# The first two weight loads of a decode block change queues, and one of them is issued in two pieces

## The chip, the cores and the metric

The kernel runs on one core of a Trainium2 chip. The metric is the device time of one execution in microseconds (us), the median of the timed runs. On the core, TensorE (PE), VectorE (DVE), ScalarE (ACT), GpSimd (POOL) and SyncE (SP) each have their own instruction stream. Data comes from the chip's main memory (HBM) into the on-chip memory SBUF, which has 128 partitions, by 16 DMA engines. SP and ACT each issue transfers into a queue of their own; the profile calls SP's queue q1 and ACT's q10.

## The reference

One decode step of a transformer block for 4 sequences (one new token each, width 512, float32), with the modulation of an adaptive layer norm:

```python
mod = (_silu(c) @ w_mod).reshape(c.shape[0], 6, 1, -1)
sa, ca, ga, sb, cb, gb = (mod[:, n] for n in range(6))
h = _layernorm(x) * (1 + ca) + sa
x = x + ga * _A_ref(h, A_k_cache, A_v_cache, A_wq, A_wo)
h = _layernorm(x) * (1 + cb) + sb
x = x + gb * _B_ref(h, B_w1, B_w3, B_w2)
# _A_ref: q = h @ wq (32 heads of 128); 8 key/value heads, the last 2048 positions of
#         the cache; softmax(q k / sqrt(128)) v; the heads' outputs @ wo
# _B_ref: (silu(h @ w1) * (h @ w3)) @ w2, inner width 1792
```

In all the kernel reads 101 MB, of which wq is 8.3 MB and the first part of w_mod (the columns for sa and ca, with x and c beside them) 2.1 MB.

## The kernel before

The host lays all inputs out as tiles of 128 partitions, so that each load is one wide transfer. SBUF holds a `ring` of three slots of 65,536 bytes for each partition. The loads go through it in a fixed order that is written out by hand:

- `w_mod_a` (128 rows of 16,512 bytes) into slot 0 and `wq` (128 rows of 64,576 bytes) into slot 1, both at the start;
- `guests`: the last 240 columns of wq, which are left out of the `wq` tile, as 24 rows of 5,760 bytes into the tile `p_sb`, in eight transfers of three rows. In each transfer the rows go to partitions four apart (`c`, `c+4`, `c+8`, or these plus 32). They wait for Pool's memset of `p_sb`;
- `kv_in[0]` to `kv_in[6]` (keys and values of one key/value head for all four sequences, 128 rows of 65,536 bytes) into slots 2, 0, 1, 2, ..., each issued when the slot's last reader is done;
- `wo_mod`, `last_k_wo`, `last_v`, `wo`, `w1`, `w3` and four pieces of `w2` into freed parts of the ring.

All loads but `wq` are issued by SP in that order; `wq` is issued by ACT (`queue="scalar"`). The helper is

```python
def load(dst, src, cuts=(0, 1), queue="sync"):
    step = src.shape[1] // cuts[-1]
    for lo, hi in zip(cuts[:-1], cuts[1:]):
        do(queue, "dma_start", dst[:, lo * step : hi * step], src[:, lo * step : hi * step])
    return dst[:, : src.shape[1]]
```

The computation follows the loads. When w_mod_a has landed, ACT and DVE form silu(c) (tiles `e`, `sc`), Pool copies x (`xs`), PE transposes and averages it and multiplies `sc` with w_mod_a (`bank<-ring,sc`); DVE makes the normalised, modulated `h`, and PE its transpose `hT`. From here slot 0 is free and `kv_in[1]` is issued. Then PE multiplies `hT` with wq (`s_ps<-ring,hT`), and slot 1 is free for `kv_in[2]`. Eight groups follow, one for each key/value head: scores (`s_ps<-ring,qT`), maximum (`nm`), exponential (`p_sb`), transposes, product with the values (`o_ps`). Then come the projection with wo, the second norm, and the gated layer with w1, w3 and w2.

`Program` (`do(...)`) records every operation with the SBUF and PSUM ranges that it reads and writes, works out the waits itself, and emits the instructions for each engine in the recorded order. For that reason nearly every instruction carries the one line L59 in the profile, and rows are told apart by their tiles. Each transfer has a semaphore of its own.

Of the kernel before, what the change touches and what calls it, by code (L numbers as in the profile page):

```python
# [9 lines left out]
P = 128  # L10
# [137 lines left out]
def block_kernel(nc, w_mod_a, wq, guests, kv_in, wo_mod, last_k_wo, last_v, wo, w1, w3, w2, out):  # L148
# [5 lines left out]
    do = Program(nc)  # L154
# [8 lines left out]
    slots = [ring[:, n * 2 * HALF : (n + 1) * 2 * HALF] for n in range(3)]  # L163
# [10 lines left out]
# [5 lines that stand above are left out]
# [4 lines left out]

    first = load(slots[0], w_mod_a)
    wma, xt_sb, ct_sb = first[:, :4096], first[:, 4096:4112], first[:, 4112:]
    wq_t = load(slots[1], wq, queue="scalar")
    do("scalar", "preload_act_table_set", "natural_log_exp_and_others")
    kv = [None] * G  # L190

# [347 lines left out]
```

## Time and profile before

| What | Value |
|---|---|
| timed runs | 242.05, 242.22, 242.52 us; median 242.22 |
| the profiled execution | span 240.8 us from its first to its last instruction; the median is 1.4 us above it |
| PE busy | 148.7 us, 62% |
| DVE, ACT, POOL busy | 56.3, 24.1, 4.5 us |
| SP's queue (q1) | 92.99 MB, 89.8% of 16 DMA engines' span |
| ACT's queue (q10) | 8.27 MB, 8.0% |
| read from HBM | 101.22 MB, 420 GB/s over the span |
| from issue to landing | w_mod_a 26.7 us, wq 26.9 us |

The profiled execution has no time of its own outside its span; the runs' times hold the span and what lies around it. The shares of the queues say how long their packets kept the 16 DMA engines busy, as a part of 16 times the span. The chain that ended last is 60% DMA, 31% PE, 5% DVE and 3% ACT. In views of a stretch, a DMA packet is counted where it starts.

### The profile page before, as it was taken

The numbers are of one execution on the slowest core, as the hardware profiler recorded it, in microseconds if no ns is written. First come the engines' busy times: TensorE is split into PE (matmuls) and PEld (weight loads), VectorE is DVE, ScalarE is ACT, GpSimd is POOL, SyncE is SP. The second block draws the span as 40 slices with busy tenths as digits, with TensorE's granted clock in tenths as the row PEclk, the third lists the DMA queues.
The fourth block names the chain that finished last, engine by engine and source line by source line (L and its number), as shares of the span: only waits on it lengthen the run. The fifth ranks groups of instructions, "written<-read, shape, count | busy, mean of one in ns | idle before, by whom it ended". The sixth has DMA issues, their size and how long they took to land.

```text
span 240.8 us, 2502 instructions
## 1 busy us (share of the span) xinstructions
PE 148.7 (62%) x1113; PEld 54.2 (22%) x1113; DVE 56.3 (23%) x141; ACT 24.1 (10%) x36; POOL 4.5 (2%) x12
## 2 busy tenths in 40 slices
PE   0000169982984962944867576667399719965876
PEld 0000133322322212201312222221042202422333
DVE  5000231034152024123132133130313104113210
ACT  2000000003003003001100300300200001320100
POOL 7000000000000000000000000000000000000000
PEclk9999997997696798879797799795759968995899
DMA  8999999999999999999999999999999999999994
GB/s 305 434 444 455 424 425 446 416 446 414 457 395 468 403 459 414 449 425 446 425 446 427 435 435 435 435 427 446 425 446 425 411 419 430 386 444 443 401 413 162
DMA packets 2937, 101.39 MB, mean 421 GB/s; under 512 B 472, under 2 KB 472, under 8 KB 880
## 3 DMA queue, kind: packets, MB, share of 16 engines
q1 hardware_dynamic: 2784, 92.99, 89.8%
q10 hardware_dynamic: 144, 8.27, 8.0%
q8 instruction: 8, 0.13, 0.2%
q14 instruction: 1, 0.01, 0.0%
HBM read 101.22 MB, written 0.03 MB: 420 GB/s over the span
## 4 chain that ended last, share of the span: by engine, by line
DMA 60%; PE 31%; DVE 5%; ACT 3%; issue 1%; ACTq 0%
DMA ring<-kv_in 33%; DMA ring<-w 16%; PE s_ps L59 14%; DMA ring<-w_mod_a 11%; PE bank L59 9%; PE o_ps L59 6%; DVE nm L59 3%; ACT p_sb L59 3%; PE a_ps L59 1%; DVE mod_a L59 0%; ACT work L59 0%; DVE p_sb L59 0%; DVE e L59 0%; DVE h L59 0%; DVE sq L59 0%
## 5 line engine op out<-in xcount | busy, mean ns | idle before, releaser
L59 PE MATMUL s_ps<-ring,qT 128*32 128x512 f32 x256 | 36.5, 722 | 20.3 <-DMA ring<-kv_in 13.3
L59 PE MATMUL bank<-ident,p_sb 128*128 128x128 f32 (+1 forms) x136 | 27.7, 353 | 30.8 <-ACT p_sb L59 30.7
L59 PE MATMUL o_ps<-ring,pT 128*16 128x512 f32 x256 | 38.4, 707 | 0.1
L59 PEld LDWEIGHTS bank<-ident,p_sb 128*128 128x128 f32 (+1 forms) x136 | 19.8, 178 | 52.5 <-ACT p_sb L59 31.7
L59 ACT ACTIVATE p_sb<-s_ps,nm 128x2048 f32<-128x2048 f32 (+1 forms) x11 | 16.5, 1501 | 139.7 <-DVE oT L59 104.1
L59 DVE TENSOR_REDUCE nm<-s_ps 128x1 f32<-128x2048 f32 x7 | 16.0, 2292 | 32.5 <-PE s_ps L59 32.5
L59 DVE COPY pT<-bank 128x64 f32<-128x64 f32 x32 | 7.2, 225 | 57.0 <-PE bank L59 57.0
L59 PEld LDWEIGHTS s_ps<-ring,qT 128*32 128x32 f32 x256 | 8.7, 129 | 46.9 <-issue 20.1
L59 PE MATMUL bank<-ident,xs 128*128 128x128 f32 x1 | 0.5, 476 | 27.8 <-POOL xs L59 27.8
L59 PE MATMUL s_ps<-ring,h2T 128*32 128x512 f32 (+1 forms) x64 | 9.0, 657 | 2.3 <-DMA ring<-w 2.3
L59 PE MATMUL s_ps<-ring,hT 128*32 128x512 f32 (+1 forms) x64 | 9.4, 705 | 0.0
L59 PEld LDWEIGHTS o_ps<-ring,pT 128*16 128x16 f32 x256 | 5.4, 99 | 11.9 <-issue 9.0
L59 DVE SCALAR_TENSOR_TENSOR o_own<-o_ps,rl,own 128x512 f32<-128x512 f32 x7 | 5.3, 751 | 11.1 <-PE o_ps L59 11.1
L59 PE MATMUL a_ps<-ring,oT 128*4 128x512 f32 x64 | 7.4, 592 | 0.0
L59 DVE TENSOR_REDUCE o_sum<-o_own 128x128 f32<-128x512 f32 x7 | 7.2, 1034 | 0.2
L59 PE MATMUL bank<-ring,sc 128*32 128x256 f32 (+1 forms) x64 | 6.9, 587 | 0.0
L59 PEld LDWEIGHTS bank<-ident,xs 128*128 128x128 f32 x1 | 0.2, 183 | 27.8 <-POOL xs L59 27.8
L59 DVE TENSOR_SCALAR e<-e 128x16 f32<-128x16 f32 x1 | 0.2, 175 | 23.3 <-ACT e L59 23.3
L59 DVE COPY qT<-bank 128x64 f32<-128x64 f32 x8 | 2.2, 280 | 12.4 <-PE bank L59 12.0
L59 DVE TENSOR_REDUCE mx<-s_ps 128x1 f32<-128x512 f32 x4 | 2.8, 692 | 9.0 <-PE s_ps L59 9.0
L59 PEld LDWEIGHTS s_ps<-ring,h2T 128*32 128x32 f32 x64 | 2.6, 130 | 7.3 <-issue 4.4
L59 PE MATMUL s_ps<-ring,hidT 128*32 128x64 f32 (+1 forms) x112 | 3.6, 274 | 0.3 <-DVE hidT L59 0.3
(97 smaller groups left out, 63.7 us busy)
## 6 DMA issues: line engine op xcount, KB each, us to landing
ring<-wq ACTq DMA_DIRECT2D x1, 8072.0 KB, 26.9
ring<-w SPq DMA_DIRECT2D x2, 3584.0 KB, 37.9
ring<-last_k_wo SPq DMA_DIRECT2D x1, 6144.0 KB, 30.1
ring<-last_v SPq DMA_DIRECT2D x1, 4096.0 KB, 39.5
ring<-w_mod_a SPq DMA_DIRECT2D x1, 2064.0 KB, 26.7
ring<-wo SPq DMA_DIRECT2D x1, 2048.0 KB, 41.8
ring<-w SPq DMA_DIRECT2D x1, 2048.0 KB, 43.1
ring<-w SPq DMA_DIRECT2D x1, 768.0 KB, 44.5
```

The source lines that it names most:

```text
L59: op = Op(engine, lambda: getattr(getattr(self.nc, engine), method)(*args, **kw), [])
```

## The change

SP now issues wq, in two transfers: the first 16 partitions, and then the other 112. ACT issues w_mod_a. Both happen at the start, ahead of everything else on the two queues. What is loaded, and to which addresses, stays the same.

```diff
-    first = load(slots[0], w_mod_a)
+    wq_t = slots[1][:, : wq.shape[1]]
+    for lo, hi in ((0, 16), (16, P)):
+        do("sync", "dma_start", wq_t[lo:hi], wq[lo:hi])
+    first = load(slots[0], w_mod_a, queue="scalar")
     wma, xt_sb, ct_sb = first[:, :4096], first[:, 4096:4112], first[:, 4112:]
-    wq_t = load(slots[1], wq, queue="scalar")
     do("scalar", "preload_act_table_set", "natural_log_exp_and_others")
```

On SP, at the start of the program, the transfers stand like this, with a minus as they were and with a plus as they are now (tile written, tensor read, partitions x elements):

```order
@@ -1,3 +1,4 @@
-L59 DMA ring<-w_mod_a 128x4128
+L59 DMA ring<-wq 16x16144
+L59 DMA ring<-wq 112x16144
 L59 DMA p_sb<-guests 3x1440 x8
 L59 DMA ring<-kv_in 128x16384 x7
```

The guests and the key/value loads now stand behind two transfers of wq on SP's queue instead of one of w_mod_a.

On ACT, also at its start (the table load is for the exponential; `e` is the first work that reads w_mod_a's tile):

```order
@@ -1,3 +1,3 @@
-L59 DMA ring<-wq 128x16144
+L59 DMA ring<-w_mod_a 128x4128
 L59 ACT_TABLE_LOAD
 L59 ACTIVATE e<-ring 128x16
```

The one transfer on ACT's queue is now w_mod_a. The other engines' instructions stand as they did; PE's first product with `hT` waits for two transfers of wq where it waited for one.

## The prediction

> **What bounds the kernel now.** I read the page's slices first, then the stretches of the span, then the chain and the DMA issues. The slices and queues of the page:
>
> ```profile
> span 240.8 us, 2502 instructions
> DMA  8999999999999999999999999999999999999994
> q1 hardware_dynamic: 2784, 92.99, 89.8%
> q10 hardware_dynamic: 144, 8.27, 8.0%
> ```
>
> q1 is SP's queue, q10 ACT's, which carries wq alone. Together their packets fill 97.8% of what 16 DMA engines have in the span. The stretches (third column from the right: granted TensorE clock; then DMA share and GB/s; a packet counts where it starts, so a short stretch can show over 1):
>
> ```profile
> 0.00:1.70 1.70, 0.00 (x0) 0.00 (x0) 0.73 (x3) 0.55 (x1) 0.94 (x7) 1.00 0.00 0
> 28.20:47.00 18.80, 15.52 (x120) 6.26 (x120) 3.68 (x15) 1.06 (x3) 0.00 (x0) 0.91 1.00 433
> 47.00:181.00 134.00, 90.01 (x568) 31.72 (x566) 35.94 (x66) 15.01 (x15) 0.00 (x0) 0.82 1.00 433
> 181.00:229.00 48.00, 34.08 (x263) 11.78 (x259) 11.38 (x36) 5.32 (x14) 0.00 (x0) 0.86 0.99 423
> 237.70:240.80 3.10, 1.09 (x64) 0.75 (x53) 0.45 (x2) 0.00 (x0) 0.00 (x0) 1.00 0.05 11
> ```
>
> Nothing moves for 1.7 us; then the engines run without a gap, at 433 GB/s (27.1 GB/s each), until the last weights have come at 237.7, and 3.1 us of work follow. So the kernel is one stream of 101 MB, and a microsecond that the DMA engines lose anywhere in it is a microsecond at the end, because no later stretch has idle time to win it back. The chain ends the same way: it hands over from transfer to transfer, and its first and last long pieces are
>
> ```profile
> 0.73 26.68 DMA ring<-w_mod_a
> 190.94 38.54 DMA ring<-w
> ```
>
> The change touches the first of them. Its two transfers, in the timeline and in the list of issues:
>
> ```profile
> 0.73 0.39 ACTq L59 DMA_DIRECT2D ring<-wq  x1
> 0.73 0.38 SPq L59 DMA_DIRECT2D ring<-w_mod_a  x1
> 3.23 5.67 SPq L59 DMA_DIRECT2D p_sb<-guests  x8
> 8.95 25.57 SPq L59 DMA_DIRECT2D ring<-kv_in  x2
> ring<-wq ACTq DMA_DIRECT2D x1, 8072.0 KB, 26.9
> ring<-w_mod_a SPq DMA_DIRECT2D x1, 2064.0 KB, 26.7
> ```
>
> Both land after the same 27 us though one is a quarter of the other. The DMA view of a stretch of 3 us, typical for 5 to 26 us, says why:
>
> ```profile
> DMA packets 32, 1.30 MB, mean 432 GB/s; under 512 B 0, under 2 KB 0, under 8 KB 0
> q10 hardware_dynamic: 16, 1.03, 79.5%
> q1 hardware_dynamic: 16, 0.26, 20.5%
> ```
>
> Each engine carries eight rows (partitions) of each tile and takes one row from one queue, then one from the other. A wq row of 64,576 bytes takes 79.5% of 3.0 us, 2.38 us; a w_mod row 0.61 us; eight pairs are 24 us.
>
> **The change, part by part.** Sums are against the profiled execution, 240.8 us; the median of the timed runs, 242.22, stands 1.4 above it, and I add that at the end.
>
> *Issues.* SP issues one transfer more. An issue costs SP 0.38 us, and SP had nothing to do between 1.11 us and the guests at 3.23, which wait for Pool's memset of p_sb: zero, and 0.4 us for the guests and kv_in if that cover were gone. Even then the guests stand behind 20 us of rows on the same queue. ACT issues w_mod_a in place of wq, one for one: zero.
>
> *Order on the engines.* wq, guests and kv_in now share SP's queue, w_mod_a is alone on ACT's. Rows still alternate, so eight pairs still take 24 us and both tiles land together: zero for the landing. kv_in's second load, issued when w_mod's slot is free (8.95 + 25.57 = 34.5 us), has 13 us in hand, as the first keeps the engines busy to about 47.5 (28.2 plus eight rows of 2.42, a kv_in row being 65,536 bytes at 27.1 GB/s). PE's product with hT waits for two transfers of wq instead of one; they end together.
>
> *The start.* The first 5.3 us, in the DMA view (40 slices of 0.13 us):
>
> ```profile
> DMA  0000000000000998030099999900000000000000
> q10 hardware_dynamic: 16, 1.03, 49.8%
> q1 hardware_dynamic: 16, 0.26, 19.8%
> ```
>
> SP's rows start in the fourteenth slice, at 1.7 us, 0.6 us after its issue ended at 1.11; ACT's follow at 2.65. The first w_mod row takes 1.05 us (19.8% of 5.3) instead of 0.61, the first wq row 2.64 instead of 2.38. A transfer of 16 rows could start its rows earlier than one of 128; at most the 0.6 us is to be won. ACT's w_mod rows may come a microsecond late, but the engines have a wq row of 2.4 us by then. I take zero and keep -0.6 for the range.
>
> *The 16 rows.* This is the term that decides. The nearest narrow transfers are the guests, eight of three rows, whose rows stand four partitions apart. The DMA view of 27.1 to 28.1 us holds four of them alone (slices of 25 ns):
>
> ```profile
> GB/s 0 0 0 0 461 231 0 0 0 0 0 0 0 461 231 0 0 0 0 0 0 0 461 231 0 0 0 0 0 0 0 461 231 0 0 0 0 0 0 0
> DMA packets 25, 0.07 MB, mean 69 GB/s; under 512 B 13, under 2 KB 13, under 8 KB 25
> q1 hardware_dynamic: 25, 0.07, 17.2%
> ```
>
> Every 0.22 us three rows of 5,760 bytes start together: each of three engines carries one row. Twelve rows take 17.2% of 16 engine-microseconds, 0.23 us each with the 13 short signal packets counted in, or 25 GB/s: full pace. So I expect 16 rows to go to 16 engines, one each, and 112 to go seven to an engine.
>
> Then all 16 engines write 16 neighbouring partitions at once, a case of which this trace has no row. If engines don't hinder each other there, a row takes 2.38 us: no cost. If partitions share a way into the memory, the guests bound the sharing: rows four apart ran side by side at full pace, so at most four neighbours share one. Four engines on one way take 4 x 2.38 = 9.5 us for their rows, and all 16 engines are held alike, since an engine finishes a row before it takes one of the other queue: +7.1 us. Between 0 and +7.1 I take +7.1: the pace per engine is the same 25 to 27 GB/s for rows of 5.8, 16.5 and 64.6 KB, which looks like a fixed width on each path rather than a common limit at the source, and 128 rows on 16 engines give each path eight partitions of its own.
>
> [...]
>
> *The 112 rows.* Suppose that engine e carries rows 16+7e to 22+7e in order, and that a path's eight partitions are two groups of four, 32 apart. At the first step the engines are at rows 16, 23, 30 ... 121: rows 16 and 51 meet on one path, and 72 and 107. Counted over all seven steps an engine needs between 7 and 10 row times for its seven rows. The latest engine decides when a tile has landed: 3 x 2.38 = +7.1. w_mod's eight rows (4.9 us) stretch on these paths by the same 10 to 7: +2.1. The ends for this part are 0, no meetings, and +50, if the rows were dealt out in turn so that sixteen neighbours are always under way (7 x 7.1).
>
> Sum: 240.8 + 7.1 + 7.1 + 2.1 = 257.1 us; with 1.4 us around it 258.5. All later tiles have 128 rows, so the lag stays what it is.
>
> **Rivals.**
> 1. *The first piece collides, the second doesn't.* Seven rows to an engine may be dealt so that paths stay apart. 242.2 + 7.1 = 249.3. For it: the 128-row tiles run at full pace, however they are dealt. Against: a count of 112 does not split into 16 equal sets of whole groups of four.
> 2. *No collisions: nothing changes.* Bytes, rows per engine and landing order are the same; 242.2. For it: no row of the trace shows an engine held up by another. Against: no row shows a narrow piece of neighbouring rows at full pace either.
> 3. *Faster: the small first transfer starts the stream sooner* and nothing collides. Place: the dead time from 1.11 to 1.7 us. It is worth up to 0.6 us, 241.6, and counts from 0.48 us on. For it: every microsecond at the start is one at the end. Against: ACT's 128 rows came 0.95 us after SP's, which need not shorten with fewer rows on SP.
> 4. *The 112 rows are dealt out in turn:* 242.2 + 7.1 + 50 = 299. Against: in the guests' view one transfer's rows start together on three engines, which fits either way of dealing.
>
> [...]
>
> **How the numbers follow.** Collisions in both pieces 0.57, in the first alone 0.13, dealt in turn 0.04: slower 0.74. No change 0.13. Shorter start 0.13. A run of this kernel tells 0.2%, 0.48 us, from no change. For the likeliest case alone the range is 250 to 264: its low end has few meetings in the second piece, its high end engines that drift out of step and meet longer, by half as much again of the 9.2 us of the second piece. The range to hold 8 in 10 leaves out the shorter start and the turn-wise dealing (0.17) and reaches from no change, 241.8, to 264.
>
> **What would show it.** Collisions: wq and w_mod_a land 10 to 20 us later than 27 us; in the first 12 us SP's queue moves some 110 GB/s; the stretch 47 to 181 keeps 433 GB/s; the tail after the last weights stays 3.1 us. First piece alone: slow to about 11 us, then 432 GB/s. No change: landings at 27 us. Shorter start: first packets well before 1.7 us. I am wrong if the 16 wq rows take 2.4 us each while all engines write neighbours.

## The result, and the profile after

The changed kernel takes 266.46 us (median of 4 runs, 266.07 to 267.08) where the kernel before takes 242.22 (242.05 to 242.52). The ratio is 1.1004, 95% interval 1.0991 to 1.1017: 24.2 us slower. The forecast was slower, 258.5 us, with a range up to 264; the direction and the place are right, the size is 8 us short.

The page of the changed kernel (span, the DMA engines' busy share in 40 slices of 6.6 us, what they moved, the two queues):

```profile
span 264.7 us, 2503 instructions
DMA  9987988899989998999999999999999999999992
GB/s 156 236 196 231 323 211 216 318 455 465 438 386 436 475 438 386 437 465 418 426 426 455 406 428 446 455 406 428 446 455 404 389 455 408 418 442 433 412 406 86
q1 hardware_dynamic: 2800, 99.14, 94.1%
q10 hardware_dynamic: 144, 2.11, 3.2%
```

Read the two slice rows together. The engines count as busy from the start, as before, but in the first eight slices (53 us) they move 156 to 323 GB/s instead of some 430. A row that reads "busy" therefore doesn't say that work is done at full pace; the GB/s row does. The stretches of the changed kernel put the loss into its place (the last two columns are DMA share and GB/s):

```profile
0.00:1.70 1.70, 0.00 (x0) 0.00 (x0) 0.73 (x3) 0.54 (x1) 0.94 (x7) 1.00 0.00 0
1.70:12.60 10.90, 0.00 (x0) 0.00 (x0) 2.65 (x15) 0.74 (x1) 3.33 (x5) 1.00 1.00 143
12.60:50.40 37.80, 0.00 (x0) 0.00 (x0) 0.00 (x0) 0.00 (x0) 0.00 (x0) 1.00 1.02 263
72.00:205.00 133.00, 91.32 (x583) 33.02 (x582) 36.38 (x69) 15.01 (x15) 0.00 (x0) 0.81 1.00 432
261.50:264.70 3.20, 1.16 (x66) 0.94 (x64) 0.45 (x2) 0.00 (x0) 0.00 (x0) 1.00 0.05 12
```

The stream starts at 1.7 us, as before. Up to 12.6 us, while the first 16 rows of wq and 32 of w_mod's 128 are under way, it runs at 143 GB/s; up to 50.4, with the other 112 rows, at 263. From there it has its old pace of 432, and the tail after the last weights is 3.2 us against 3.1. Nothing later gives the loss back. The issues of the changed kernel (KB each, us from issue to landing):

```profile
ring<-wq SPq DMA_DIRECT2D x1, 1009.0 KB, 12.2
ring<-wq SPq DMA_DIRECT2D x1, 7063.0 KB, 50.4
ring<-w_mod_a ACTq DMA_DIRECT2D x1, 2064.0 KB, 50.6
```

The first 16 rows need 12.2 us and both tiles 50 instead of 27: 23.5 and 23.9 us later, and the end is 24.2 us later. PE and DVE do the same work as before (148.6 and 56.3 us busy); they begin later.

How fast single rows go shows in a DMA view of a short stretch of the changed kernel. The first 16 rows of wq are those of 1.7 to 12.6 us (q1's other 16 packets are short signals):

```profile
q1 hardware_dynamic: 32, 1.03, 77.4%
q10 hardware_dynamic: 32, 0.53, 22.6%
```

77.4% of 10.9 us on 16 engines, over 16 rows, are 8.4 us a row. The first rows of the 112 start between 12.65 and 17.6 us:

```profile
DMA packets 32, 1.30 MB, mean 262 GB/s; under 512 B 0, under 2 KB 0, under 8 KB 0
q1 hardware_dynamic: 16, 1.03, 88.0%
q10 hardware_dynamic: 16, 0.26, 21.2%
```

Sixteen wq rows take 88.0% of 4.95 us on 16 engines, 4.36 us each instead of 2.38; sixteen w_mod rows 1.05 us instead of 0.61. Between 23.4 and 26.4 us it is otherwise:

```profile
DMA packets 29, 1.25 MB, mean 416 GB/s; under 512 B 0, under 2 KB 0, under 8 KB 0
q1 hardware_dynamic: 16, 1.03, 98.8%
q10 hardware_dynamic: 13, 0.21, 23.5%
```

Here a wq row takes 2.96 us on the mean, but the trace's single packets show that 14 of the 16 rows take 2.7 us and two take 4.9 and 5.1. In the stretch behind it, 26.7 to 31.6 us, that pace is gone again (80.0% of 4.9 us, 3.92 us a row):

```profile
q1 hardware_dynamic: 16, 1.03, 80.0%
```

So the 112 rows aren't slow evenly. Taken sixteen at a time in the order of their starts, they have means of 4.36, 4.42, 2.96, 3.92, 4.56, 4.48 and 4.22 us by the packets: one step runs at nearly full pace, six at little more than half. The experiments say why.

### The profile page after: what moved, and what is told of

It reads as the page before. It is cut to its first block, busy times and chain, and to the rows that moved or that the text cites. A ratio compares the mean times of both kernels' runs of the same rounds, so it can differ in the third digit from the quotient of the medians.

```text
span 264.7 us, 2503 instructions
## 1 busy us (share of the span) xinstructions
PE 148.6 (56%) x1113; PEld 55.0 (21%) x1113; DVE 56.3 (21%) x141; ACT 24.1 (9%) x36; POOL 4.5 (2%) x12
## 4 chain that ended last, share of the span: by engine, by line
DMA 46%; PE 27%; another core or an unknown queue 18%; DVE 4%; ACT 3%; issue 0%; ACTq 0%
DMA ring<-wo_mod 16%; DMA ring<-w 15%; DMA ring<-kv_in 15%; PE s_ps L59 11%; PE bank L59 8%; PE o_ps L59 6%; DVE nm L59 3%; ACT p_sb L59 3%; PE a_ps L59 1%; ACT L59 0%; DVE mod_a L59 0%; ACT work L59 0%; DVE p_sb L59 0%; DVE e L59 0%
## 5 line engine op out<-in xcount | busy, mean ns | idle before, releaser
L59 PE MATMUL s_ps<-ring,qT 128*32 128x512 f32 x256 | 35.4, 703 | 19.1 <-DMA ring<-kv_in 10.8
L59 PE MATMUL bank<-ident,p_sb 128*128 128x128 f32 (+1 forms) x136 | 28.4, 359 | 30.8 <-ACT p_sb L59 30.7
L59 PEld LDWEIGHTS bank<-ident,p_sb 128*128 128x128 f32 (+1 forms) x136 | 20.6, 184 | 52.7 <-ACT p_sb L59 31.7
## 6 DMA issues: line engine op xcount, KB each, us to landing
ring<-wq SPq DMA_DIRECT2D x1, 7063.0 KB, 50.4
ring<-wq SPq DMA_DIRECT2D x1, 1009.0 KB, 12.2
```

The source lines that it names most:

```text
L59: op = Op(engine, lambda: getattr(getattr(self.nc, engine), method)(*args, **kw), [])
```

## The experiments

Theory P is that of the prediction: engines that write partitions of one path into SBUF at the same time share its pace; a path, as it supposes, serves four neighbouring partitions and the four that lie 32 on. No trace names the path of a packet, so the pairs that meet are counted by this grouping; the landings of the single transfers below fit it (sixteen rows: 5.0 and 5.1 us without a pair, 6.5 to 7.3 with one to eight pairs). The rivals are Q (the new order on the queues costs), S (reading in HBM costs), N (any narrow piece costs), C (a second or small first transfer costs), M (the engines are only set out of step) and, later, H (engines that meet also hold up those that don't).

**Swap and split apart.** The swap alone (the changed kernel without the split):

```diff
-    wq_t = slots[1][:, : wq.shape[1]]
-    for lo, hi in ((0, 16), (16, P)):
-        do("sync", "dma_start", wq_t[lo:hi], wq[lo:hi])
+    wq_t = load(slots[1], wq)
```

> SP issues wq whole (128 partitions), ACT issues w_mod_a: the change without the split. Theory P (engines that write neighbouring partitions share a way into SBUF, so the split costs): as before, 242.2 us within 0.5; both tiles land 27 us after their issue. Rival Q (what costs is wq standing ahead of the guests and kv_in on SP's queue): 266 us as in the changed kernel.

Measured: 242.38 us, ratio to before 1.0012 (1.0000 to 1.0024); wq lands after 27.1 us, w_mod_a after 27.2. The swap costs nothing that can be told. The split alone, on the old queues (against the kernel before):

```diff
-    wq_t = load(slots[1], wq, queue="scalar")
+    wq_t = slots[1][:, : wq.shape[1]]
+    for lo, hi in ((0, 16), (16, P)):
+        do("scalar", "dma_start", wq_t[lo:hi], wq[lo:hi])
```

> ACT issues wq as 16 and 112 partitions, SP issues w_mod_a: the split without the swap. Theory P: 266 us within 1.5, landings near 50 us. Rival Q: 242 us. Rival S (the reading side in HBM is slowed by the rows that the engines read together, not the writing side): 266 too; it is told apart by the probe.

Measured: 266.37 us, ratio 1.0995 (1.0977 to 1.1014). The split is the whole cost, on either queue. Q falls.

**Two halves.** Against the changed kernel:

```diff
-    for lo, hi in ((0, 16), (16, P)):
+    for lo, hi in ((0, 64), (64, P)):
```

> The changed kernel with wq in two pieces of 64 partitions instead of 16 and 112. Theory P with paths of eight partitions (four neighbours and the four 32 on): 64 partitions reach 8 of 16 paths, two engines on each, so a wq row takes 4.8 instead of 2.4 us: 8 x 2.4 = +19 us, and up to +5 where w_mod rows meet them: 261 to 266 us. Rival N (only narrow pieces of 16 rows are slow): 243 us or less. Rival S: the 16 engines read 16 rows two apart, much like the whole tile: 242 to 245 us.

Measured: 264.51 us, ratio 1.0925 (1.0906 to 1.0944), 22.3 us slower. Broad pieces of 64 partitions are slow too, by what P says for 8 paths. N falls as it was put here. S does not expect it, but the next run decides.

**Reading or writing.** Eight transfers of 16 rows, one at a time, ahead of the unchanged program (the list of partitions is left out):

```diff
...
+        op = do("sync", "dma_start", slots[2][a0:a1:a2, :wide], wq[b0:b1:b2, :wide])
+        op.waits.append(last_probe)
...
```

> Eight transfers of 16 wq rows (64.6 KB each, a little narrower from one to the next) run one at a time ahead of the unchanged program, into the slot of kv_in[0], with different partitions written and different rows read: (1) written 0-15, read 0-15; (2) written 0-15, read every fourth row; (3) written every fourth, read 0-15; (4) written every eighth, read 0-15; (5) written every seventh from 16, read 0-15; (6) written and read every seventh from 16; (7) the same from 18; (8) written every seventh from 18, read every seventh from 16. Times are from issue to landing, with about 2 us around the rows. Theory P: 1 and 2 alike at 11.5 us; 3 and 4 at 6.8; 5 and 6 alike, 6.8, set by the two pairs of engines that meet, the other twelve rows at 2.4 us; 7 and 8 the same by one pair. Rival S: 2 differs from 1, 3, 4 and 5 are like 1. Rival H (one meeting pair holds up engines that do not meet): in 5 and 6 all 16 rows take over 4 us.

Measured (issues of this kernel in the order of the list; each is 8 KB smaller than the one ahead of it, which tells them apart):

```profile
ring<-wq SPq DMA_DIRECT2D x1, 1009.0 KB, 11.5
ring<-wq SPq DMA_DIRECT2D x1, 1001.0 KB, 11.5
ring<-wq SPq DMA_DIRECT2D x1, 993.0 KB, 7.3
ring<-wq SPq DMA_DIRECT2D x1, 985.0 KB, 7.3
ring<-wq SPq DMA_DIRECT2D x1, 977.0 KB, 6.9
ring<-wq SPq DMA_DIRECT2D x1, 969.0 KB, 6.9
ring<-wq SPq DMA_DIRECT2D x1, 961.0 KB, 6.7
ring<-wq SPq DMA_DIRECT2D x1, 953.0 KB, 6.7
```

The first two read different rows and write the same partitions: 11.5 and 11.5. The first and the third read the same rows and write differently: 11.5 and 7.3. Transfers 5 and 6, and 7 and 8, say the same. What is read doesn't matter; S falls. The landings are as P forecast, 0 to 0.5 us off. But the view of transfer 5 alone (39 to 46 us of this kernel; partitions 16, 23, ... 121)

```profile
DMA packets 32, 1.00 MB, mean 143 GB/s; under 512 B 16, under 2 KB 16, under 8 KB 16
q1 hardware_dynamic: 32, 1.00, 57.1%
```

gives 57.1% of 7 us, 4.0 us a row over all sixteen, where P has twelve rows at 2.4 and four at 4.8, a mean of 3.0. Transfer 7, from partition 18, where one pair meets by the grouping, had 46.0% of 6.9 us (53 to 59.9 us), 3.2. The landing alone hides the difference, as it is that of the last row. A mean of 4.0 us in transfer 5 is what H expected. The 3.2 us of transfer 7 are not: there one pair meets, and H had one pair hold up all. The eleven and ten transfers further on take this apart.

**The two pieces apart.** An extra copy of the 16 rows, ahead of wq whole (in the kernel of the swap alone):

```diff
+    do("sync", "dma_start", slots[2][:16, : wq.shape[1]], wq[:16])
     wq_t = load(slots[1], wq)
```

> The swapped kernel with wq whole, and ahead of it on SP a copy of wq's first 16 rows into partitions 0-15 of the slot of kv_in[0] (1.03 MB more). Theory P: only this piece collides; it takes 9.2 to 9.5 us of all engines: 242.4 + 9.3 = 251.7 us within 1. Rival M (the piece itself is cheap, and what costs is that it sets the engines out of step with w_mod's rows): 242.4 + 2.4 = 244.8 us.

Measured: 251.36 us, ratio 1.0378 (1.0363 to 1.0393). That is 9.0 us above the swapped kernel. The same copy into spread partitions:

```diff
-    do("sync", "dma_start", slots[2][:16, : wq.shape[1]], wq[:16])
+    do("sync", "dma_start", slots[2][32:93:4, : wq.shape[1]], wq[:16])
```

> As the run with the extra copy of wq's first 16 rows, but the copy goes to every fourth partition from 32 to 92 instead of 0 to 15. By the grouping (four neighbours and the four 32 on, in each half of 64) these 16 partitions lie on 16 paths. Theory P: the copy costs its bytes alone, 2.4 us: 242.4 + 2.4 = 244.8 us within 0.7. Rival N (any piece of 16 rows is slow): 251.4 us as with the neighbours.

Measured: 244.88 us, ratio 1.0110 (1.0093 to 1.0127), 2.5 us above the swapped kernel: the bytes and no more. The same 16 rows from the same place, to 16 other partitions, are 6.5 us cheaper. N and M fall for the first piece. The second piece alone, with Pool's zeros in place of the first (against the changed kernel):

```diff
-    for lo, hi in ((0, 16), (16, P)):
+    for lo, hi in ((16, P),):
...
+    do("gpsimd", "memset", wq_t[:16], 0.0)
```

> The changed kernel without the transfer of the first 16 rows of wq (Pool fills them with zeros instead, so 2.4 us of rows are missing and q is not the reference's). Theory P with my count (the slowest engine needs 10 row times for seven rows, w_mod stretched alike): 242.4 - 2.4 + 9.2 = 249.2 us. Theory H (engines that meet hold up those that don't, so nearly every row of the second piece and every w_mod row takes 1.7 to 1.9 times as long): 242.4 - 2.4 + 17 = 257 us within 1.5.

Measured: 256.14 us, ratio 1.0581 (1.0567 to 1.0595). The swapped kernel less the 2.4 us of the rows left out is 240.0, so the second piece costs 16.1 us more than its bytes: H's number, not that of my count. Pool's zeros are no part of it: they are written by 18.5 us, and wq and w_mod_a land 41 and 44 us after their issue.

**Cut by columns.** Against the changed kernel:

```diff
-    for lo, hi in ((0, 16), (16, P)):
-        do("sync", "dma_start", wq_t[lo:hi], wq[lo:hi])
+    for lo, hi in ((0, 2018), (2018, 16144)):
+        do("sync", "dma_start", wq_t[:, lo:hi], wq[:, lo:hi])
```

> The changed kernel with wq cut by columns instead of by partitions: 2018 columns of all 128 partitions (the same 1.03 MB), then the other 14126. Theory P: no collisions, 242.4 us within 0.5, as for wq whole. Rival C (it is the second transfer or the small first one that costs, whatever its partitions): clearly over 245 us. If a smaller first transfer starts the stream sooner, up to 0.6 us under.

Measured: 243.12 us, ratio 1.0043 (1.0028 to 1.0059). The same bytes in two transfers, with all 128 partitions in each, cost 0.7 us against wq whole, more than the half that I allowed; C falls as an account of the 24 us, and where the 0.7 comes from was not followed. One more thing is to be seen in its issues:

```profile
ring<-w_mod_a ACTq DMA_DIRECT2D x1, 2064.0 KB, 10.8
ring<-kv_in SPq DMA_DIRECT2D x7, 41.4
```

w_mod_a lands 16 us earlier than before, since its rows alternate with the short rows of the first piece (8,072 bytes each; it lands after 10.6 us), and the time isn't better. That fits a stream without gaps, which gains nothing from an earlier landing; with the 0.7 us unexplained, this run doesn't show by itself that the gain is zero.

**When lone engines are held up.** Eleven and then ten transfers like those above, with 8 to 16 partitions chosen for the number of pairs that meet:

> Eleven transfers, one at a time, ahead of the unchanged program, into the slot of kv_in[0]; rows read are always the first of wq. Eight partitions from 0 in steps of (1) four, (2) five, (3) seven, (4) one, (5) two; sixteen in steps of seven from (6) 17, (7) 19, (8) 20, (9) 0, (10) 18, (11) 16. Eight rows go to eight engines. Theory P, with eight partitions to a path: (1) nobody meets, rows of 2.4 us, 4.7 us from issue to landing; (2) and (3) one pair meets, two rows of 4.4 and six of 2.4; (4) two paths for four engines each, 11.5; (5) four paths for two, 7.3. Theory H: in (2) and (3) the six others are slowed too, clearly over 3 us. For sixteen: (6), (8), (11) have two pairs, one in each half of the partitions, (9) two pairs in the lower half, (7) and (10) one pair. If two pairs hold up all engines, mean rows are near 4 us in (6), (8), (11) and near 3 in (7) and (10); (9) tells whether the halves matter.

> Ten transfers, one at a time, ahead of the unchanged program, into the slot of kv_in[0]; rows read are the first of wq. Sixteen partitions in steps of four from (1) 32, (2) 28, (3) 24, (4) 20, (5) 16; (6) sixteen in steps of seven from 11; (7) eight in steps of three from 0; (8) twelve in steps of four from 28; (9) twelve in steps of three from 35; (10) fourteen in steps of four from 48. By the grouping the pairs of engines that meet are: (1) none, (2) one, (3) two, (4) three, (5) four, (6) none, (7) two of eight engines, (8) one, (9) two, (10) two. Theory P: rows of 2.4 to 2.9 us and a landing under 5.5 us in (1) and (6), the others 6.5 to 7. Theory H with a threshold of two pairs (as the second probe suggests for 16 engines): mean rows near 3 us in (2) and (8), near 4 in (3), (4), (5), (9), (10), and in (7) too if the number of engines does not matter. If instead the hold-up grows pair by pair, the mean climbs evenly from (1) to (5).

A row's mean time is the share in a view of its stretch, times the stretch, times 16 engines, over its rows (the signal packets weigh some 0.01 us each in the traces of the two kernels). For instance, in the last kernel, transfers (2), in 7.0 to 13.6 us, and (3), in 13.6 to 20.7:

```profile
q1 hardware_dynamic: 32, 1.03, 44.5%
...
q1 hardware_dynamic: 32, 1.02, 63.2%
```

| Engines, pairs that meet | Partitions | Mean row, us |
|---|---|---|
| 16, none | from 32 in steps of 4; from 11 in steps of 7 | 3.0; 2.8 |
| 16, one | from 28 in steps of 4; from 19 and from 18 in steps of 7 | 2.9; 3.0; 3.0 |
| 16, two | from 24 in steps of 4; from 17, 0, 20 and 16 in steps of 7 | 4.5; 4.3; 4.2; 4.2; 4.0 |
| 16, three and four | from 20 and from 16 in steps of 4 | 4.5; 4.3 |
| 8, none | from 0 in steps of 4 | 3.0 |
| 8, one | from 0 in steps of 5; of 7 | 3.1; 3.2 |
| 8, two | from 0 in steps of 3 | 4.0 |
| 8, four | from 0 in steps of 2 | 4.3 |
| 8, four engines on each of two paths | from 0 in steps of 1 | 7.9 |
| 12, one | from 28 in steps of 4 | 3.0 |
| 12, two | from 35 in steps of 3 | 4.0 |
| 14, two | from 48 in steps of 4 | 4.1 |

(The rows of a lone transfer are some 0.5 us longer than the 2.38 us of the running stream: 2.8 to 3.0 with nobody meeting.) The landings of the ones with 16 engines in the last kernel, in the order none, one, two, three, four pairs, and none:

```profile
ring<-wq SPq DMA_DIRECT2D x1, 1009.0 KB, 5.1
ring<-wq SPq DMA_DIRECT2D x1, 1001.0 KB, 6.6
ring<-wq SPq DMA_DIRECT2D x1, 993.0 KB, 7.1
ring<-wq SPq DMA_DIRECT2D x1, 985.0 KB, 7.0
ring<-wq SPq DMA_DIRECT2D x1, 977.0 KB, 6.9
ring<-wq SPq DMA_DIRECT2D x1, 969.0 KB, 5.0
```

Sixteen partitions that lie on sixteen paths by the grouping land in 5.0 and 5.1 us, the sixteen neighbours of the first probe in 11.5. The step from 32 to 28 puts partition 28 in place of 92, and by the grouping it shares a path with 60; that one exchange makes one slow pair and a landing of 6.6 us.

Means alone don't say which rows were slow, but the trace's single packets do. In transfer (2), with one pair, 14 rows take 2.4 to 2.9 us and two take 4.2: one meeting pair slows itself alone. In transfer (3), with two pairs, all 16 rows take 4.0 to 5.1 us. So with two pairs every row goes slow, at about two thirds of the pace that the rows of a lone transfer have where nobody meets (4.0 to 4.5 us against 2.8 to 3.0), whether 8, 12, 14 or 16 engines are at work; three, four and (transfers 3 and 4 of the first probe, 4.4 us a row) eight pairs add nothing. H as it was put, with one pair enough, falls; it holds with a threshold of two pairs. Why two pairs slow everybody and one doesn't was not settled: no run here looks behind the write.

## Why the prediction was right or wrong

- *One stream, any loss is a loss at the end:* right. Both tiles land 23.5 to 23.9 us later, the end is 24.2 us later, the stretch 72 to 205 us keeps 432 GB/s, the tail 3.2 us. The landings lie beyond the 10 to 20 us that the prediction gave as a sign.
- *Issues, order on the engines, a shorter start at zero:* right. The swap alone is 242.38 us; the stream of the changed kernel starts at 1.7 us as before.
- *The 16 rows, +7.1:* right in cause and nearly in size. The copy to neighbours costs 9.0 us, the one to spread partitions 2.5: +6.5 for the meeting; in the changed kernel such a row takes 8.4 us where four in turn would take 9.5. No row of the trace before showed the sharing: the +7.1 was the upper end of a bound, chosen by argument. The 1.03 MB of the copy in its 9.0 us are 115 GB/s.
- *The 112 rows, +7.1, and w_mod's rows, +2.1:* this is the term that was mis-sized. It measured +16.1 where it stood at 9.2. The failed step is "an engine needs between 7 and 10 row times for its seven rows": it let an engine be slowed only by the one that it meets. What the runs showed in its place is that from two pairs on all engines are slowed. In the run of the second piece alone, an engine's seven wq rows take 29.6 us by the trace's packets where 16.7 is full pace, +12.9 for the +7.1, and its eight w_mod rows 8.6 instead of 4.9, +3.7 for the +2.1 (together 16.6, near the 16.1 by time). That a path's two groups of four lie 32 apart was supposed, and no row of the trace before shows it; the single transfers fit it, as the experiments say. By this grouping and the dealing that the prediction supposed, five of the seven steps (from partitions 16, 17, 20, 21, 22) have two pairs and two steps (18 and 19) have one. In the changed kernel's first step a wq row takes 4.36 us and a w_mod row 1.05, together 2.4 us more than the 3.0 us of the two at full pace; five such steps are 12 us, and the two others bring the rest. The fast stretch at 23.4 to 26.4 us is the first of the two, with just one pair of slow rows, as the count has it. The second of them, at 3.92 us, isn't fast. Its pair begins from 26.8 us on, while the late pair of the step before is on its rows until 28.5 and 28.8, so that two pairs may be under way at a time; that reading is argued, not tested.
- *How rows are dealt:* 16 rows that go to neighbours at once take 8.4 us each, and those of the 112 take 3.9 to 4.6 on the mean in the slow steps; that, and the one fast step, fit seven rows in a run to each engine. A whole tile can't be dealt in such runs: eight in a run would have eight pairs in every step by the grouping, and its rows take 2.38 us. No run shows how it is dealt.
- *The range to 264:* its top let engines that drift out of step meet longer, half as much again of the second piece. The runs show another reason, the hold-up from two pairs on, and a larger one; drift shows at most in the step at 3.92 us.
- The two pieces measured by themselves make 242.38 + 6.5 + 16.1 = 265.0; the remaining 1.5 us, the first and the second piece one behind the other, were not tested.
- *Rivals:* the first piece alone (249.3) falls with the second piece's 16.1 us, no change and the shorter start with the result, dealing in turn (299) with the 4.4 us rows.

## What to carry to other kernels

Split a load by columns, or not at all, before splitting it by partitions: a piece that doesn't span the 128 partitions evenly can run well below the pace (here 115 GB/s for 16 neighbours and 263 in the stretch of the 112, against 432), and it holds up whatever else is on the same engines (w_mod's rows took 1.05 us beside the first rows of the 112, instead of 0.61). Where a piece must be narrow, choose its partitions (here 32 to 92 in steps of four, which cost 2.5 us where sixteen neighbours cost 9.0) so that the engines don't meet. When pricing a collision of two pairs or more, price it for everybody on the engines (here 4.0 to 4.5 us a row instead of 2.8 to 3.0), not for those alone that meet, and read GB/s beside the busy share: an engine that is held up counts as busy (here a share of 1.00 at 143 GB/s).

## What the runs showed of the hardware that I had not expected

Two pairs of engines that write on shared paths, as the grouping counts them, slow every engine's rows to a mean of 4.0 to 4.5 us, those that meet nobody included; with one pair the mean over all rows, the pair's included, is 2.9 to 3.2 us, against 2.8 to 3.0 where nobody meets. Two pieces of 64 partitions are nearly as dear (+22.3 us) as 16 and 112 (+24.2). And a landing 16 us earlier for w_mod_a, in the kernel cut by columns, made the kernel no faster (+0.7 us against wq whole).
